# A float32 attention and GLU block on one core: the second token pair takes its 64 leftover rows into the seven products (49 matmuls a chunk for 50), and VectorE's sum of two partial results becomes an accumulation in PSUM

## The chip, the core and the metric

The kernel runs on one core of a Trainium2 chip. The engines of that core work side by side: TensorE (PE; its weight loads are listed apart as PEld) multiplies matrices and writes to PSUM, VectorE (DVE) and ScalarE (ACT) do elementwise work, GpSimd (POOL) does small tensor work and issues some of the transfers, and SyncE (SP) issues the other transfers. Each engine takes its instructions in a fixed order, which the builder of the program has laid down, and waits at an instruction until the semaphores that it needs are set. The metric is the device time of one execution in microseconds (us).

## What is computed

```python
x = A_x                                            # 1 x 2048 x 576, float32
h = x + A_ref(layernorm(x), wqkv, wo)              # 32 heads of 18, 8 keys at distance 2 behind each token
h2 = h + B_ref(layernorm(h), w_gate, w_up, w_down)

def B_ref(x, w_gate, w_up, w_down):                # 576 -> 4608 -> 576
    g = x @ w_gate
    u = x @ w_up
    return (sigmoid(g) * u) @ w_down
```

## The kernel before, in words

**Precision.** Every float32 operand of a large product is split into a high part that TensorE can take (`float32r`) and the low part that is left over: ScalarE copies the high part (L104), VectorE subtracts it from the source (L105). A product of two such operands takes three matmuls: high with high, low with high, high with low.

**Blocks and chunks.** The 2048 tokens are four blocks of 512. The 4608 hidden columns are 36 chunks of 128. The 576 input rows are four tiles of 128 and 64 rows over, the rest. For the rest the 64 rows stand twice in the 128 partitions, as high part and as low part, and two matmuls with the weights' high and low part cover it.

**Four stages of the second half.** The list `items` runs over 12 chunks of block 0 alone ("std"), 24 chunks of blocks 0 and 1 together (the first pair), 12 chunks of block 2 alone, and all 36 chunks of blocks 2 and 3 together (the last pair). In a pair, gate and up of two blocks are four outputs, and the function `pair` makes them by a scheme of seven products of half the inner length in place of eight: sums and differences of the operands are multiplied, and partial results are shared. The products are called by the names of their weights: b00, b10, t2, t3, t1, t4, b11. Each product is two tiles of 128 rows times three matmuls, 6 matmuls of 128 x 512 (`prod`, L747); the rests of the four outputs are added outside the scheme, by 4 x 2 matmuls (`rest`, L754). That makes 7 x 6 + 8 = 50 a chunk.

**Around the products.** The results stand in three PSUM tiles, b1, b2 and b3. ScalarE copies partial results out of them (L824, L834, L838), VectorE adds others to these copies (L829, L843, L848), ScalarE takes the sigmoid, and VectorE multiplies gate by up (L767; in the last pair L1187). In the last pair the down projection runs over two chunks at a time with seven products of its own (`down_seven`, L930: 14 steps of 6 matmuls of 128 x 288 for each half of the tokens in two chunks, results to the tile ev by ScalarE at L936, added to a buffer in HBM by transfers that GpSimd issues at L939). The other stages use `down_tile` (L868; PSUM tile dp), whose results ScalarE (L876) or VectorE (L878) take out.

**Preparing the operands.** The weights of the next chunk are prepared while this one runs (`weights`: four splits, and three subtractions at L727, L728, L730, from the tile wg that SyncE loads at L702). The operands of the last pair come from blocks 2 and 3, whose attention output is projected and normalised in the background of the third stage (`under_rest`, `proj_scr`, ending with ScalarE's writes to the tile ar at L978). From them `operands` makes the sums s1 to s4 (L281 to L287, and the rest's difference rd at L289) and splits seven operands, three of them with a rest (L108, L109).

**What sets the order.** The code is written as generators that are stepped between products (`between`, `bg_step`, `units`); priorities (HC above HI above none) and a list scheduler lay down each engine's order when the program is built. Buffers of a tile rotate: a new tile waits until the readers of the one that stood in its place are done.

## Time and profile before

| | |
|---|---|
| median of 3 runs | 1567.01 us (1566.04 to 1567.74) |
| profiled execution | 1568.13 us, of which 1566.4 us from the first to the last instruction |
| granted TensorE clock | 0.999 |
| PE busy / PEld busy | 1542.5 us / 1373.7 us |
| DVE busy / ACT busy / POOL busy | 1253.5 us / 874.0 us / 207.1 us |
| moved | 273.96 MB, 175 GB/s |

The span is a little shorter than the execution's time, since the time has the start and the end of the program in it as well. "Busy" is the union of an engine's instructions. Matmuls overlap in the records: one of 128 x 512 is listed with 391 ns, while the next one starts about 0.23 us after it. A line of groups gives the source line, engine, operation, output and inputs, shapes and count, then busy time and the mean of one instruction in ns, and behind the second bar the idle time of the engine just before them and what ended it.

### The profile page before, as it was taken

Reading aid. Unit: us, or ns where it says so; the run is one execution under the profiler, and the core shown is the slowest. Engines: PE = TensorE matmul, PEld = TensorE weight load, DVE = VectorE, ACT = ScalarE, POOL = GpSimd, SP = SyncE. Lnnn points to the kernel's source line nnn. Section 1 sums busy time; section 2 is a strip of 40 time slices with the busy share of each in tenths; the row PEclk is TensorE's granted clock in tenths of the full one; section 3 lists DMA queues with packets and bytes.
Section 4 is the critical chain, followed back from the end, with each engine's and each line's share of the span. In section 5 each row is a group of like instructions: output and inputs, shape, how many; then the busy total and the mean of one; then the engine's idle time right before and its main releaser. Section 6 shows DMA issues by size and latency. Waiting matters only on the chain.

```text
span 1566.4 us, 22385 instructions
## 1 busy us (share of the span) xinstructions
PE 1542.5 (98%) x8520; PEld 1373.7 (88%) x8520; DVE 1253.5 (80%) x1880; ACT 874.0 (56%) x1584; POOL 207.1 (13%) x252
## 2 busy tenths in 40 slices
PE   8999999999999999999999999999999999999998
PEld 7899888887888888888888888888888888888888
DVE  6998999969999999999526588866777776677754
ACT  6632245435656555666542355766677766677761
POOL 2300000011000110001101010112121121111212
PEclk9999999999999999999999999999999999999999
DMA  8646545266566776665683424898888889888984
GB/s 279 211 173 211 202 186 192 100 220 212 121 186 167 184 183 160 165 161 117 170 243 128 175 81 127 186 189 177 167 177 190 183 164 191 177 161 187 190 167 136
DMA packets 77148, 273.96 MB, mean 175 GB/s; under 512 B 8336, under 2 KB 14224, under 8 KB 76144
## 3 DMA queue, kind: packets, MB, share of 16 engines
q0 software_dynamic: 28192, 107.29, 37.4%
q1 hardware_dynamic: 41216, 145.11, 27.0%
q10 hardware_dynamic: 7632, 20.12, 3.4%
q8 instruction: 66, 1.08, 0.3%
q14 instruction: 42, 0.34, 0.1%
HBM read 143.98 MB, written 130.87 MB: 175 GB/s over the span
## 4 chain that ended last, share of the span: by engine, by line
PE 83%; DVE 8%; DMA 5%; ACT 1%; issue 1%; POOL 0%; ACTq 0%; SPq 0%; POOLq 0%; DVEq 0%
PE b L747 41%; PE dp L868 15%; PE dp L930 11%; PE b L754 8%; PE acc L157 4%; DMA wg<-in_wmlp_dram 2%; DVE pr L189 1%; DVE lg L193 1%; DVE pr L215 1%; PE b L157 1%; PE bgp L157 1%; DMA kw<-k 1%; DMA x<-tok 1%; DMA k<-ev 1%; DVE w L105 0%
## 5 line engine op out<-in xcount | busy, mean ns | idle before, releaser
L747 PE MATMUL b<-tl,w 128*128 128x512 f32 x1692 | 423.4, 392 | 1.6 <-ACT s L824 1.0
L747 PEld LDWEIGHTS b<-tl,w 128*128 128x128 f32 x1692 | 307.6, 188 | 59.7 <-ACT s L824 1.5
L747 PE MATMUL b<-th,w 128*128 128x512 f32 x1332 | 341.4, 391 | 0.4 <-DVE s L843 0.4
L747 PEld LDWEIGHTS b<-th,w 128*128 128x128 f32 x1332 | 246.0, 188 | 48.9 <-DVE s L843 0.8
L754 PE MATMUL b<-th,w 128*128 128x512 f32 x564 | 174.6, 390 | 0.0
L939 POOL DMA_DIRECT2D h<-ev x128 | 109.2, 853 | 455.9 <-ACT ev L936 451.0
L104 ACT ACTIVATE w<-wg 128x384 fp32r<-128x384 f32 (+1 forms) x186 | 111.0, 600 | 91.2 <-PE b L754 47.3
L157 PE MATMUL acc<-qw,th 128*128 128x432 f32 x512 | 154.3, 362 | 3.1 <-DVE th L109 2.3
L936 ACT ACTIVATE ev<-dp 128x576 f32<-128x576 f32 x224 | 139.0, 648 | 22.0 <-PE dp L930 22.0
L105 DVE TENSOR_TENSOR w<-wg,w 128x384 fp32r<-128x384 f32 (+1 forms) x186 | 120.9, 655 | 37.3 <-ACT w L104 37.1
L105 DVE TENSOR_TENSOR w<-tw,w 128x512 fp32r<-128x512 f32 x120 | 82.5, 688 | 79.6 <-ACT w L104 79.3
L754 PEld LDWEIGHTS b<-th,w 128*128 128x128 f32 x564 | 105.9, 188 | 22.5
L104 ACT ACTIVATE w<-tw 128x512 fp32r<-128x512 f32 x120 | 75.6, 630 | 83.4 <-PE b L747 82.3
L868 PE MATMUL dp<-d,h1h 128*128 128x288 f32 x640 | 118.8, 295 | 0.0
L868 PE MATMUL dp<-d,h0h 128*128 128x288 f32 x608 | 112.3, 295 | 0.0
L876 ACT ACTIVATE stage<-dp 128x576 f32<-128x576 f32 x104 | 66.9, 646 | 68.3 <-PE dp L868 68.1
L157 PEld LDWEIGHTS acc<-qw,th 128*128 128x128 f32 x512 | 96.7, 189 | 8.8 <-DVE th L109 3.4
L868 PEld LDWEIGHTS dp<-d,h1h 128*128 128x128 f32 x640 | 98.8, 189 | 3.0
L868 PEld LDWEIGHTS dp<-d,h0h 128*128 128x128 f32 x608 | 94.0, 189 | 3.5 <-DVE stage L878 0.3
L157 PE MATMUL acc<-qw,tl 128*128 128x432 f32 x256 | 92.8, 362 | 0.1
L189 DVE TENSOR_TENSOR pr<-kw,q 128x2304 f32<-128x2304 f32 x32 | 81.8, 2556 | 10.9 <-DMA kw<-k 10.7
L884 POOL DMA_DIRECT2D h<-stage x26 | 31.1, 1197 | 416.6 <-ACT stage L876 337.6
(323 smaller groups left out, 2971.6 us busy)
## 6 DMA issues: line engine op xcount, KB each, us to landing
h<-ev POOLq DMA_DIRECT2D x96, 576.0 KB, 7.1
wg<-in_wmlp_dram SPq DMA_DIRECT2D x47, 928.0 KB, 5.2
h<-stage POOLq DMA_DIRECT2D x26, 1152.0 KB, 11.7
wg<-in_wmlp_dram SPq DMA_DIRECT2D x36, 640.0 KB, 5.3
kw<-k SPq DMA_DIRECT2D x16, 792.0 KB, 5.1
vw<-v SPq DMA_DIRECT2D x16, 792.0 KB, 5.1
wd<-in_wmlp_dram SPq DMA_DIRECT2D x18, 576.0 KB, 8.1
h<-ev POOLq DMA_DIRECT2D x32, 288.0 KB, 5.1
```

What stands on the lines that cost most here:

```text
L104: act.activation(hi, src, AF.Copy)
L105: splits.append(dve.tensor_tensor(lo, src, f32(hi), ALU.subtract))
L157: pe.matmul(ps[:, :n], a[:, c, js], m[:, c], start=k == 0, stop=False)
L189: dve.tensor_tensor(pr, both(kw, u), q[:, us].unsqueeze(2).broadcast_to([P, 2, W, CG]), ALU.mult)
L747: pe.matmul(ps, wt[:, a, k0 + c], xx[:, m + c], start=first and k == 0, stop=k == 5, skip_group_check=True)
L754: pe.matmul(ps, wt[:, a, k0], xx[:, 4], start=False, stop=a == 1, skip_group_check=True)
L868: pe.matmul(ps[:, i, :DH2], a[:, js], d[:, m, i * DH2:(i + 1) * DH2], start=k == 0, stop=k == n)
L876: act.activation(hv, ps, AF.Copy)
L884: pool.dma_start(hacc[b], hs, accum_op=ALU.add, max_dma_last_dim=8 * D)
L930: pe.matmul(ps[:, i, :DH2], a[x][:, js], m[y], start=k in (0, 1, 3) and q == 0, stop=q == 2, skip_group_check=True)
L936: act.activation(hs[:, k % 2], ps[:, :, :DH2], AF.Copy)
L939: pool.dma_start(hsev[:, u, k0:k + 1], hs[:, :k + 1 - k0], accum_op=ALU.add, max_dma_last_dim=8 * D)
```

## The change

- Only the last pair is given new weights and operands. The 64 rows of the rest are cut into two halves of 32 rows, one for each half of the inner length, and so take part in the scheme of seven products. In the 128 partitions the token operand of a rest holds its 32 rows as high, low, high, high; the weight operand holds high, high, low, low, of which the last is zero, so that one matmul gives the three terms. Each product is 6 + 1 matmuls: 7 x 7 = 49 a chunk (`product`, `full_weights`).
- A second packing of the weights, `wfull`, is an input of its own, with 12 x 128 columns a chunk in place of 10 x 128. The preparation of a chunk's weights works in place in the loaded tile, with six copies on ScalarE and twelve operations on VectorE for four and seven.
- The seven operands of the last pair each have a rest. The rest rows of blocks 2 and 3 are written to HBM (`rscr`, GpSimd's queue, 2 transfers of 128 KB) and read back into four tiles rr00 to rr11, the 32 rows four times over (16 transfers of 64 KB on the same queue). `x_full` and `split_quads` split each rest with one copy on ScalarE and one subtraction on VectorE of 32 partitions.
- In both pairs the products stand in another order: b00, t3, t2, b10, t1, t4, b11. From the second chunk of each pair on, ScalarE copies b00's result from one PSUM tile into the other (the new L895), the matmuls of b10 (eight in the first pair, seven in the last) accumulate on top of it, and the sigmoid reads PSUM; VectorE's addition L829 is gone there. The first chunk of each pair keeps the addition (the new L910).
- Buffers: s has 3 for 4, ev has 3 for 4, d3 has 1 for 2. The rests of the token operands have a pool of their own. A chunk's first copy of weights waits for the last sigmoid of the chunk before it.

The diff, cut to its core:

```diff
+    rscr = [dr.tile([DR, TB], F32, name=f"r{b}") for b in (2, 3)]
...
+    def split_quads(t, src):
+        act.activation(t, src, AF.Copy)
+        dve.tensor_tensor(t[32:64], src[32:64], f32(t[32:64]), ALU.subtract)
...
+    def full_weights(ws):
+        r = ws[:, :GF].rearrange("p (b c n) -> p b c n", b=4, c=3)
+
+        def quads(t, src):
+            act.activation(t, src, AF.Copy)
+            dve.tensor_tensor(t[64:128], src[64:128], f32(t[64:128]), ALU.subtract)
+
+        def sum_pair(name, q, bs):
+            t = gw.tile([P, 2, 4, P], F32R, name=name)
+            split(t[:, :, 0:2], t[:, :, 2:4], r[:, bs, 1:3])
+            quads(tr[:, q:q + 2], r[:, bs, 0])
+            return t
+
+        with tc.high_priority(HI):
+            w1 = gw.tile([P, 2, 5, P], F32R, bufs=2, name="w1")
+            with ExitStack() as way:
+                if c >= NF + NSTD:
+                    way.enter_context(tc.issue_after(added[1]))
+                act.activation(w1[:, :, 0:3], r[:, 2:4], AF.Copy)
+            dve.tensor_tensor(w1[:, :, 3:5], r[:, 2:4, 1:3], f32(w1[:, :, 1:3]), ALU.subtract)
+            dve.tensor_tensor(w1[64:128, :, 0], r[64:128, 2:4, 0], f32(w1[64:128, :, 0]),
+                              ALU.subtract)
+            dve.tensor_tensor(r[:, 1], r[:, 0], r[:, 1], ALU.subtract)
+            dve.tensor_tensor(r[:, 2], r[:, 1], r[:, 2], ALU.add)
+            dve.tensor_tensor(r[:, 3], r[:, 3], r[:, 2], ALU.subtract)
+            tr = gw.tile([P, 8, P], F32R, tag="tw", name="tr")
+            w2 = sum_pair("w2", 0, slice(1, 3))
+            w4 = gw.tile([P, 6, P], F32R, name="w4")
+            act.activation(w4[:, 0:3], r[:, 0], AF.Copy)
+            dve.tensor_tensor(w4[:, 3:5], r[:, 0, 1:3], f32(w4[:, 1:3]), ALU.subtract)
+            dve.tensor_tensor(w4[64:128, 0], r[64:128, 0, 0], f32(w4[64:128, 0]), ALU.subtract)
+            dve.tensor_tensor(r[:, 0], r[:, 0], r[:, 2], ALU.subtract)
+            w3 = sum_pair("w3", 2, slice(0, 4, 3))
...
+    def product(ps, n, xn, w, first, rests):
+        prod(ps, X[xn], w, n, first)
+        if isinstance(w[n][1], int):
+            for m, wn in rests:
+                rest(ps, X[m], w, wn)
+        else:
+            pe.matmul(ps, w[n][1], XR[xn], start=False, stop=True, skip_group_check=True)
...
-        prod(b1, X["a00"], w, "b00", True)
+        product(b1, "b00", "a00", w, True, ())
         with tc.high_priority(HC):
-            act.activation(s1, b1, AF.Copy)
+            act.activation(b2 if clean else s1, b1, AF.Copy)
         between(0)
-        prod(b2, X["a01"], w, "b10", True)
-        rest(b2, X["a01"], w, "g4")
+        product(b3, "t3", "s3", w, True, ())
...
+        product(b2, "b10", "a01", w, not clean, (("a01", "g4"),))
         with tc.high_priority(HC):
-            act.activation(s3, b3, AF.Copy)
+            if clean:
+                act.activation(s1, b2, AF.Sigmoid)
+            else:
+                dve.tensor_tensor(s1, s1, b2, ALU.add)
+                act.activation(s1, s1, AF.Sigmoid)
...
+        elif b > 1:
+            pool.dma_start(rscr[b - 2], raw[0:DR, 4])
...
+            rr = [[pp.tile([P, TB], F32, name=f"rr{i}{h}") for h in range(2)] for i in range(2)]
+            for i in range(2):
+                for h in range(2):
+                    a = rscr[i][32 * h:32 * h + 32, :]
+                    for q in range(4):
+                        pool.dma_start(rr[i][h][32 * q:32 * q + 32], a)
+                    yield
...
-                    hs = st.tile([P, 2, 2, DH2], F32, bufs=4, name="ev")
+                    hs = st.tile([P, 2, 2, DH2], F32, bufs=3, name="ev")
```

Three places show what the change does to the order of an engine's instructions. (In these lists w1 to w4 are the split weights of a chunk, tr their rests for t1 to t4, th and tl operands with and without a rest, xa00 and xs1 to xs3 the new rests of the token operands; the number behind a name tells one tile from the next of the same name.)

**TensorE in a chunk of the last pair.** Before, the second chunk, whole: b00 in the bank b2_9212, b10 in b3_9213, and so on, with four rests of two matmuls.

```order
L747 MATMUL b2_9212<-tl_8832,w1_9031 128x512 x6
L747 MATMUL b3_9213<-th_8835,w1_9031 128x512 x6
L754 MATMUL b3_9213<-th_8835,w1_9031 128x512 x2
L747 MATMUL b2_9212<-tl_8892,w2_9035 128x512 x6
L747 MATMUL b1_9214<-tl_8895,w2_9035 128x512 x6
L747 MATMUL b2_9212<-tl_9019,w3_9036 128x512 x6
L754 MATMUL b2_9212<-th_9022,w4_9034 128x512 x2
L747 MATMUL b1_9214<-th_9022,w3_9036 128x512 x6
L754 MATMUL b1_9214<-th_9022,w1_9031 128x512 x2
L747 MATMUL b2_9212<-th_8904,w4_9034 128x512 x6
L754 MATMUL b2_9212<-th_8904,w4_9034 128x512 x2
```

Now, the end of the second chunk (t2, b10, t1, t4, b11) and the first product of the third:

```order
L808 MATMUL b1_9251<-tl_8901,w2_9065 128x512 x6
L818 MATMUL b1_9251<-xs2_8902,tr_9064 128x512
L808 MATMUL b2_9253<-th_8913,w1_9057 128x512 x6
L818 MATMUL b2_9253<-th_8913,w1_9057 128x512
L808 MATMUL b1_9251<-tl_9042,w3_9075 128x512 x6
L818 MATMUL b1_9251<-xs1_9043,tr_9064 128x512
L808 MATMUL b3_9252<-th_9048,w3_9075 128x512 x6
L818 MATMUL b3_9252<-th_9048,tr_9064 128x512
L808 MATMUL b1_9251<-th_8933,w4_9070 128x512 x6
L818 MATMUL b1_9251<-th_8933,w4_9070 128x512
L808 MATMUL b2_9389<-tl_8859,w1_9226 128x512 x6
L818 MATMUL b2_9389<-xa00_8860,w1_9226 128x512
```

The pairs of rest matmuls have become one matmul behind each product.

**TensorE at the join of the third stage and the last pair.** Before, from t1 of the first chunk (bank b1_9049) to t2 of the second, where each bank is finished before the next chunk begins:

```order
L747 MATMUL b1_9049<-tl_9019,w3_8941 128x512 x6
L754 MATMUL b1_9049<-th_9022,w4_8939 128x512 x2
L747 MATMUL b3_9051<-th_9022,w3_8941 128x512 x6
L754 MATMUL b3_9051<-th_9022,w1_8936 128x512 x2
L747 MATMUL b1_9049<-th_8904,w4_8939 128x512 x6
L754 MATMUL b1_9049<-th_8904,w4_8939 128x512 x2
L747 MATMUL b2_9212<-tl_8832,w1_9031 128x512 x6
```

Now, the same place: the first chunk has the banks b1_9084, b2_9082, b3_9083, the second b1_9251 and b3_9252.

```order
L808 MATMUL b1_9251<-tl_8859,w1_9057 128x512 x6
L818 MATMUL b1_9251<-xa00_8860,w1_9057 128x512
L818 MATMUL b3_9083<-xs3_8880,tr_8959 128x512
L808 MATMUL b3_9083<-th_9048,w3_8970 128x512 x6
L818 MATMUL b3_9083<-th_9048,tr_8959 128x512
L818 MATMUL b2_9082<-xs2_8902,tr_8959 128x512
L808 MATMUL b2_9082<-tl_9042,w3_8970 128x512 x6
L818 MATMUL b2_9082<-xs1_9043,tr_8959 128x512
L808 MATMUL b3_9252<-tl_8879,w2_9065 128x512 x4
L808 MATMUL b2_9082<-th_8933,w4_8965 128x512 x6
L818 MATMUL b2_9082<-th_8933,w4_8965 128x512
L808 MATMUL b3_9252<-tl_8879,w2_9065 128x512 x2
```

The rests of t3 and t2 of the first chunk now stand behind b00 of the second chunk, each right ahead of the next product into the same bank. Behind the last row come one matmul more of the second chunk's t3 (its rest) and the first matmul of the down projection (`dp` from h0h), which needs the first chunk's gate times up.

**VectorE at the same place.** Before, from the last operand (a11, the tile th_9022) to the addition behind b10 and on:

```order
L105 TENSOR_TENSOR th_9022<-ar3_8328,th_9022 128x1024
L878 TENSOR_TENSOR stage_7678<-stage_7678,dp_9062 128x576
L105 TENSOR_TENSOR w1_9031<-wg_8952,w1_9031 128x640
L727 TENSOR_TENSOR tw_9037<-wg_8952 128x512
L829 TENSOR_TENSOR s_9052<-s_9052,b2_9050 128x512
L109 TENSOR_TENSOR th_9022<-ar3_8328,th_9022 64x512
L878 TENSOR_TENSOR stage_7678<-stage_7678,dp_9088 128x576
```

Now, from a11's rest on:

```order
L115 TENSOR_TENSOR th_9048<-rr11_8819,th_9048 32x512
L758 TENSOR_TENSOR wg_8975<-wg_8975 128x384
L107 TENSOR_TENSOR w2_9065<-wg_8975,w2_9065 128x2x256
L951 TENSOR_TENSOR stage_7657<-stage_7657,dp_9142 128x576
L756 TENSOR_TENSOR wg_9080<-wg_9080 128x384
L1108 TENSOR_TENSOR rd_8815<-rr10_8818,rr11_8819 128x512
L910 TENSOR_TENSOR s_9085<-s_9085,b1_9084 128x512
L1108 TENSOR_TENSOR rr10_8818<-rr00_8816,rr10_8818 128x512
L951 TENSOR_TENSOR stage_7657<-stage_7657,dp_9165 128x576
L115 TENSOR_TENSOR xs3_8880<-rr10_8818,xs3_8880 32x512
L115 TENSOR_TENSOR xs1_9043<-rd_8815,xs1_9043 32x512
```

The work on the rests stands behind the last operand's main part, among the sums of the down results (L878, now L951) and the weights of the second and third chunk. From the sum s1 (before L281, now rs0) up to the row of xs3 there are 52 instructions now: 9 of 1024 columns, 8 of 576, 18 of 512, 10 of 384, 6 of 256 and 1 of 128.

More of the change, by code (lines that the diff above doesn't have):

```diff
@@ L60, with kernel @@
 @with_exitstack
-def kernel(ctx, tc, x, wqkv, wo, wmlp, out):
+def kernel(ctx, tc, x, wqkv, wo, wmlp, wfull, out):
     nc = tc.nc
@@ L298, in tl_tile, with x_full @@
         return xt.tile([P, 4, TB], F32R, tag="tl", bufs=4, name="tl")
+    def x_full(n, raw, rest):
+        if n in ("a01", "a11", "s4"):
+            t = th_tile()
+            r = t[:, 4]
+        else:
+            t = tl_tile()
+            r = xr.tile([P, TB], F32R, name="x" + n)
+        split(t[:, 0:2], t[:, 2:4], raw)
+        split_quads(r, rest)
+        XR[n] = r
+        return t
+    XR = {}
+    xr = None
     def x_half(raw, rest):
@@ L698, with load_gu @@
         gw.tile([P, n, P], F32 if name == "tw" else F32R, name=name)
[L700 removed]
+    def load_gu(f, full):
         ws = gw.tile([P, WC], F32, bufs=2, name="wg")
[L702 removed]
+        n, src = (GF, wfull) if full else (WC, wmlp)
+        behind[0] = sp.dma_start(ws[:, :n], src[f][:, :n])
         return ws
@@ L746, in prod @@
             for a, m in ((0, 0), (0, 2), (1, 0)):
-                pe.matmul(ps, wt[:, a, k0 + c], xx[:, m + c], start=first and k == 0,
+                lhs = wt[:, a, k0 + c] if isinstance(k0, int) else wt[:, 2 * a + c]
+                pe.matmul(ps, lhs, xx[:, m + c], start=first and k == 0,
                           stop=k == 5, skip_group_check=True)
                 k += 1
+    def product(ps, n, xn, w, first, rests):
[5 more added lines that the diff above has]
+            pe.matmul(ps, w[n][1], XR[xn], start=False, stop=True, skip_group_check=True)
     def rest(ps, xx, w, n):
@@ L849, in pair @@
             gated[0] = act.activation(s2, s2, AF.Sigmoid)
+            added[1] = getattr(gated[0], "ins", gated[0])
         between(5)
-        prod(b1, X["s4"], w, "b11", False)
-        rest(b1, X["s4"], w, "u4")
         with tc.high_priority(HC):
-            last((s1, b1), (s2, s3))
+            last(1, s2, s3)
+        product(b1, "b11", "s4", w, False, (("s4", "u4"),))
+        with tc.high_priority(HC):
+            last(0, s1, b1)
         between(6)
@@ L1292, in between @@
                 side(i)
-            pair(X, w, between, last)
+            pair(w, between, last)
         else:
@@ L1309, in between @@
                 down_side(f, i)
-            pair(X, w, between, last if f >= NF - NPL else last_sums(f))
+            pair(w, between, last if f >= NF - NPL else last_sums(f))
             if f < NF - NPL:
```

123 lines of the change are left out of this document (79 added, 44 removed).

## The prediction

> **What bounds the kernel now.** I read the page first, then the groups and the stretches of the last pair, then its chain, then the join ahead of it.
>
> ```profile
> span 1566.4 us, 22385 instructions
> PE 1542.5 (98%) x8520; PEld 1373.7 (88%) x8520; DVE 1253.5 (80%) x1880; ACT 874.0 (56%) x1584; POOL 207.1 (13%) x252
> ```
>
> TensorE is busy for 98% of the span. Whether that is a bound must be seen in the stage that the change touches most. Of 1077 to 1281 us, twelve chunks of the last pair, the groups of TensorE say:
>
> ```profile
> L747 PE MATMUL b<-tl,w 128*128 128x512 f32 x288 | 71.8, 391 | 0.0
> L747 PE MATMUL b<-th,w 128*128 128x512 f32 x216 | 55.1, 390 | 0.0
> L754 PE MATMUL b<-th,w 128*128 128x512 f32 x96 | 29.7, 390 | 0.0
> ```
>
> 288 + 216 + 96 = 600 matmuls in 12 chunks, the 50 a chunk of the scheme, and no idle time ahead of any. Their 390 ns overlap; what one costs is read from the chain of waits, where there is nothing but matmuls in this stretch:
>
> ```profile
> 1183.80 1.60 PE dp L930 x12
> 1188.04 2.75 PE b L747 x12
> 1192.83 2.73 PE b L747 x12
> 1205.03 2.75 PE b L747 x12
> ```
>
> 2.73 / 12 = 0.2275 us for one of 128x512, 1.60 / 12 = 0.133 us for one of the down projection. 50 x 0.2275 + 42 x 0.133 = 16.97 us, and from the second row to the last, one chunk, it is 16.99 us. So a chunk of the last pair is the sum of its matmuls, with nothing else in it. The stretches (in the order PE, PEld, DVE, ACT, POOL busy, clock, DMA share, GB/s) show where that holds and where not:
>
> ```profile
> 340.00:420.00 80.00, 76.84 (x412) 65.07 (x412) 73.19 (x111) 42.97 (x73) 11.34 (x16) 1.00 0.56 172
> 920.00:940.00 20.00, 20.00 (x108) 17.51 (x108) 19.54 (x28) 11.78 (x19) 0.00 (x0) 1.00 0.21 67
> 940.00:958.00 18.00, 18.00 (x102) 15.97 (x101) 13.05 (x21) 6.54 (x12) 1.23 (x1) 1.00 0.42 120
> 958.00:990.00 32.00, 32.00 (x157) 27.23 (x157) 31.59 (x58) 22.17 (x41) 1.76 (x2) 1.00 0.56 134
> 1077.00:1281.00 204.00, 204.00 (x1107) 179.45 (x1106) 148.44 (x259) 143.14 (x259) 40.93 (x48) 1.00 0.88 178
> ```
>
> In the steady last pair (last row) TensorE is full, VectorE has 12.37 us of work in a chunk, ScalarE 11.93. At the join (rows two to four) TensorE is full too, but VectorE has only 70 - 64.2 = 5.8 us to spare from 920 to 990 us. At the head of the first pair (first row) TensorE loses 3.2 us.
>
> **Matmuls removed.** One in each of 36 chunks of the last pair: 36 x 0.2275 = 8.2 us, all on the path. The first pair keeps its 50, so its chunks cannot become shorter where TensorE is full.
>
> **Weights of a chunk in the last pair.** The prices by form, VectorE first, then ScalarE; the last ScalarE rows are from 920 to 950 us:
>
> ```profile
> L105 DVE TENSOR_TENSOR w<-tw,w 128x512 fp32r<-128x512 f32 x24 | 16.5, 689 | 28.3 <-ACT w L104 28.3
> L105 DVE TENSOR_TENSOR w<-wg,w 128x640 fp32r<-128x640 f32 x12 | 9.8, 819 | 0.0
> L829 DVE TENSOR_TENSOR s<-s,b 128x512 f32<-128x512 f32 x12 | 8.3, 688 | 10.2 <-PE b L754 9.8
> L727 DVE TENSOR_TENSOR tw<-wg 128x512 f32<-128x512 f32 x12 | 8.2, 687 | 0.0
> L105 DVE TENSOR_TENSOR w<-wg,w 128x384 fp32r<-128x384 f32 x12 | 6.6, 553 | 0.0
> L730 DVE TENSOR_TENSOR tw<-wg,tw 128x256 f32<-128x256 f32 x12 | 5.0, 419 | 0.0
> L104 ACT ACTIVATE w<-tw 128x512 fp32r<-128x512 f32 x24 | 15.2, 634 | 24.3 <-PE b L747 24.3
> L104 ACT ACTIVATE w<-wg 128x640 fp32r<-128x640 f32 x12 | 8.7, 722 | 0.0
> L824 ACT ACTIVATE s<-b 128x512 f32<-128x512 f32 x12 | 7.1, 594 | 1.7 <-PE b L747 1.7
> L104 ACT ACTIVATE w<-wg 128x384 fp32r<-128x384 f32 x12 | 6.3, 525 | 5.6 <-PE b L754 5.6
> L104 ACT ACTIVATE tl<-rs 128x1024 fp32r<-128x1024 f32 x2 | 2.1, 1054 | 1.0 <-DVE rs L283 1.0
> L104 ACT ACTIVATE w<-wg 128x256 fp32r<-128x256 f32 x1 | 0.4, 418 | 0.3 <-PE b L747 0.3
> ```
>
> VectorE loses 0.82 + 0.55 + 2 x 0.69 + 0.69 + 2 x 0.42 and the addition L829, 0.69: 4.97 us. It gains three operations of 512 columns, four of 384, and five of 256 or fewer: 3 x 0.69 + 4 x 0.55 + 5 x 0.42 = 6.37. Net +1.4, so 13.8 us in a chunk of 16.77. ScalarE loses 0.72 + 0.53 + 2 x 0.63 = 2.5 and gains 768 columns (between 0.72 and 1.05, by columns 0.83), 0.53, 2 x 0.63 and 2 x 0.42 = 3.46: 12.9 of 16.77. Both stay at about 80% and under TensorE: no cost. Their cover is the slack of a chunk; the tightest edge is tr, one buffer for four rests, free after t4 and needed by the next chunk's t3, two products and a down step later, 2 x 1.6 + 0.8 = 4.0 us, against a copy and a subtraction of 0.42 each. If that cover went, each us would cost 36 us.
>
> **Accumulation in PSUM.** The trace has no copy of ScalarE from PSUM to PSUM; nearest is L824, PSUM to SBUF, 0.59 us. Its bounds are 0.42 and 1.05 us, the ends of the ScalarE rows above. t2 waits for it behind six or more matmuls of t3, 1.37 us, so only the upper end leaves too little for the two handovers; L834 before had the same cover (t2, then t3, then t1) and made no idle time in the steady part. I take 0. VectorE's 23 additions less in the first pair, 16 us, lie beside a full TensorE and bring nothing there; only the 3.2 us lost at 340 to 420 us could shrink. Gain 3.2 at most, loss about 1.5 (half of it again, since the new order falls differently among the long attention operations); I take 0.
>
> **The join.** The last operand data is written here, and the rests then leave by GpSimd's queue:
>
> ```profile
> 919.83 0.26 ACT L978 ACTIVATE ar<-bgp 128x128 f32<-128x128 f32 x1
> 896.49 0.74 POOL L976 DMA_DIRECT2D h<-hj  x1 [35.96 <-DVE hj L262]
> h<-hj POOLq DMA_DIRECT2D x8, 288.0 KB, 2.6
> 920.02 0.42 DVE L105 TENSOR_TENSOR w<-wg,w 128x256 fp32r<-128x256 f32 x1
> 920.35 1.22 DVE L281 TENSOR_TENSOR rs<-ar 128x1024 f32<-128x1024 f32 x1
> 921.49 0.69 DVE L767 TENSOR_TENSOR s<-s,b 128x512 f32<-128x512 f32 x1
> 922.08 0.56 DVE L105 TENSOR_TENSOR w<-wg,w 128x384 fp32r<-128x384 f32 x1
> 922.55 1.22 DVE L283 TENSOR_TENSOR rs<-rs,ar 128x1024 f32<-128x1024 f32 x1
> 940.28 1.54 PE L747 MATMUL b<-tl,w 128*128 128x512 f32 x6
> ```
>
> One write and 16 reads (the first read stands ahead of the write) at 0.74 us of issue each are 17 x 0.74 = 12.6 us, and the last lands 2.6 us later: 920.1 + 12.6 + 2.6 = 935.3 us. GpSimd has nothing else to do there (0.00 in the second stretch). VectorE is the later one. From start to start an operation of 1024 columns takes 1.14 us, of 512 0.59, of 384 0.47, of 256 0.33; between them one of 576 is 0.67 and one of 128 about 0.2. The 52 instructions from the sum s1 to the rest of s3 are 9 x 1.14 + 8 x 0.67 + 18 x 0.6 + 10 x 0.47 + 6 x 0.33 + 0.2 = 33.3 us, from 920.35 to 953.7. TensorE starts the last pair at 940.28 (last row) and has in front of t3's rest three products of seven, two of six and four groups of down matmuls: 21 x 0.2275 + 12 x 0.2275 + 4 x 1.60 = 13.9 us, to 954.2. So this rest is just in time. Behind it three waits are new, because no down work is left to fill them. t4 goes into the bank of t3's rest and needs ScalarE's copy in between, 0.6 us and 0.2 for the handovers. t1 behind t2's rest, the same: 0.8. The first down matmul needs VectorE's product and ScalarE's copy behind b11, 0.69 + 0.63 + 0.25, and has three matmuls of t3 to cover it, 0.7: 0.9. Together 2.5 us. Below: nothing is to be gained, since TensorE has no idle time there before; the low end is 0. Above: VectorE has five rest splits and three sums more, 8 x 0.6 = 4.8 us, and the weights of three chunks, 3 x 1.4 and the L829 that the first chunk keeps, 4.9. That is 9.7 against 5.8 to spare, and 3.9 may come on top: 6.4 us. I take 2.5, by the three waits.
>
> **Buffers.** ev with 3 for 4: in the last pair a transfer of ev and the third tile after it stand like this, the second row being two copies of which the second opens that tile at 1197.2:
>
> ```profile
> 1189.47 0.85 POOL L939 DMA_DIRECT2D h<-ev  x1 [3.04 <-ACT ev L936]
> 1196.62 1.21 ACT L936 ACTIVATE ev<-dp 128x576 f32<-128x576 f32 x2
> h<-ev POOLq DMA_DIRECT2D x96, 576.0 KB, 7.1
> DMA to landing us min/median/max: 4.6/6.3/9.4
> q1 hardware_dynamic: 8979, 29.45, 16.4%
> ```
>
> The room is 7.7 us, the landing 7.1 in the middle and 9.4 at most, so ScalarE will sometimes wait, up to 1.7 us. TensorE needs that bank only two products and a step later, 4.0 us: no cost. The loads grow by 0.131 MB a chunk; in 1009 to 1519 us 29.45 MB took 16.4% of 510 us (last row: packets, MB, share), 2.8 us a MB: +0.37 us to 0.88 x 17.0 = 15.0 us of transfer in a chunk of 16.77, 91%.
>
> **Sum.** -8.2 + 2.5 = -5.7 us: against the profiled execution 1568.13 - 5.7 = 1562.4. The median of the runs before, 1567.01, is 1.1 us lower than that execution, so 1561.3. About 0.2%, 3.1 us, is what a measurement can tell from no change.
>
> **A rule weighed.** TensorE's weight loads are busy for 179.45 of 204 us, 88%, with no idle time before any matmul. The Trainium skill, Perfetto Trace Analysis, section Identifying the Most-Contended Engine, says that busy matmuls are a bad measure of how near TensorE is to its limit, and that the busy share of weight loads is a better one. By it 12% would be free, something else would be the bound, and a matmul less would bring nothing: 1567 in place of 1561. The chain, 16.99 us for 16.97 of matmuls, decides against it here; what is left of it is a rival.
>
> **Rivals.**
> - The join costs nothing (VectorE's rests come earlier, or the new waits overlap): 1567.0 - 8.2 = 1558.8, and with the head of the first pair repaired 1555.6. For it: the margin at 954 us is within the error of my count. Against: each new wait is in TensorE's own order.
> - The join costs its upper end, VectorE being late with all that it has over: 1567.0 - 8.2 + 6.4 = 1565.2, no change. For it: 31.59 of 32 us busy at 958 to 990.
> - The removed matmuls were not the bound, and each chunk stays at 17.0 us: 1567.0 + 2.5 = 1569.5 at most, no change. Against it: the chain.
> - Slower, by ev: if a landing goes beyond 7.7 + 4.0 - 0.65 = 11 us, TensorE waits for the bank, once in two chunks, 17 times; beyond 11.5 us, 0.52 us each time, that is 8.8 us and outweighs the 5.7 by 3.1: from there slower, at 12 us 1578. For it: a queue at 91%. Against it: 9.4 is the longest now.
> - Slower, by the rests: were each transfer to wait until the one ahead has landed, 17 x 2.6 = 44 us would put the last at 964, ten behind the need: 1571. Against it: ev's transfers are issued every 4.2 us and land after 7.1, so they overlap. The Trainium skill, DMA: Bandwidth & Descriptors, section Anatomy of one DMA, gives a fixed 2.0 us and bytes / 436e3 for one such transfer; one behind the other these would make an estimated 37 us, to 957.
>
> **Chances.** My forecast (join 1 to 4 us) 0.50; free join 0.22; dear join 0.13; not the bound 0.04; ev 0.07; rests 0.04. Faster takes the first two, 0.72; the next two are the same, 0.17; slower 0.11. The range from 1557.0 to 1566.5 holds the forecast, most of the free join and the dear join, and leaves out the two slower cases, the fourth and the gain at the first pair's head. The forecast's own range is 1559.5 to 1563.5.
>
> **What would show it.** Chunks of the last pair 16.75 us apart in the chain; 588 matmuls in twelve of them, with idle 0.0; VectorE near 13.8 and ScalarE near 12.9 us a chunk; TensorE idle for 1 to 4 us between 940 and 975, behind ACT copies of b and ahead of the first dp; the rests' reads landed by 936. ScalarE waiting on ev's transfers for some tenths of a us a chunk, and TensorE not. It is wrong if TensorE shows idle time in each chunk, or if the lost time at the join, or at the head of the first pair, is over 6 us.

## The result, and the profile after

The changed kernel is 1.3% slower: 1586.69 us median of 6 runs (1579.91 to 1592.66) against 1566.01 us, ratio 1.0133, 95% interval 1.0104 to 1.0161. The prediction was 1561.3 us. The runs spread over 13 us, those of the kernel before over 4. The profiled execution took 1592.66 us, the slowest of the six, so the stalls below are at their larger end.

The head of the page of the kernel after, and the shares of its engines in the chain of work that ended last:

```profile
span 1590.9 us, 22470 instructions
PE 1551.7 (98%) x8484; PEld 1373.8 (86%) x8484; DVE 1297.4 (82%) x2009; ACT 906.7 (57%) x1660; POOL 218.3 (14%) x270
PE 58%; DVE 24%; DMA 12%; ACT 3%; issue 2%; POOL 0%; SPq 0%; ACTq 0%; DVEq 0%; POOLq 0%
```

TensorE has 36 matmuls less (8484 for 8520) and yet 9 us more of busy time. Before the change, DMA had 5% of the chain; now it has 12%. Where that happens is seen in the stretches (PE, PEld, DVE, ACT, POOL busy, clock, DMA share, GB/s). First the kernel before: the head of the first pair, the join, the even part of the last pair. Then the same of the kernel after:

```profile
340.00:422.00 82.00, 78.84 (x424) 66.93 (x424) 75.19 (x114) 44.97 (x76) 11.34 (x16) 1.00 0.54 168
940.00:985.00 45.00, 45.00 (x231) 38.80 (x230) 39.71 (x68) 26.13 (x48) 2.14 (x2) 1.00 0.45 116
985.00:1526.00 541.00, 541.00 (x2923) 475.27 (x2922) 388.99 (x676) 376.95 (x679) 108.27 (x127) 1.00 0.89 181
```

```profile
340.00:422.00 82.00, 78.66 (x425) 66.73 (x424) 75.64 (x113) 46.00 (x78) 11.32 (x16) 1.00 0.57 177
942.00:997.00 55.00, 49.89 (x229) 40.46 (x228) 47.94 (x85) 30.03 (x56) 2.27 (x3) 0.94 0.40 106
997.00:1551.00 554.00, 543.73 (x2888) 471.64 (x2887) 437.04 (x806) 403.42 (x744) 109.06 (x127) 0.99 0.89 184
```

The first pair is as it was. The join takes 55 us for 45, with TensorE idle for 5.1 us and a clock of 0.94. The even part of the last pair takes 554 us for 541; TensorE was full there and is now idle for 10.3 us, spread over it, and runs at half its clock for 6.8 us of it.

**The even part.** Of 1009 to 1519 us, the waits of the kernel after (us in total, times, longest), and the group of L756, the first subtraction in the newly loaded weights:

```profile
DVE wg L756 <- DMA wg<-in_wfull_dram: 79.1, 25, 7.7
PEld b L808 <- DVE s L915: 6.9, 6, 2.3
PEld dp L1003 <- DVE d L107: 6.0, 7, 1.3
L756 DVE TENSOR_TENSOR wg<-wg 128x384 f32<-128x384 f32 x29 | 16.2, 558 | 79.3 <-DMA wg<-in_wfull_dram 79.1
```

VectorE stands still for 79 us at one instruction. In the kernel before no instruction of VectorE or ScalarE waited for a load of weights in this stretch. The chain at one such place, and TensorE's row there:

```profile
1137.47 9.52 DMA wg<-in_wfull_dram
1147.08 0.10 DVE wg L756
1147.56 0.69 DVE s L915
1148.29 2.05 PE b L808 x6
1148.29 2.05 PE L808 MATMUL b<-th,w 128*128 128x512 f32 x6 [2.02 <-DVE s L915]
```

The load of the weights, wg, is issued at 1137.47 us and lands 9.52 us later. L756 stands in VectorE's fixed order ahead of L915, the addition that reads the bank b1; b11 goes into that bank next, so TensorE waits 2.02 us. The transfers themselves are hardly different: from issue to landing 4.3, 5.3 and 8.7 us (least, median, most) in the kernel before, 4.1, 5.3 and 9.5 after. What changed is the time between the issue and the first reader. Before, the first reader of the load issued at 1103.86 us was a copy of ScalarE at 1115.95 us, 12.1 us later:

```profile
1103.86 0.33 SPq L702 DMA_DIRECT2D wg<-in_wmlp_dram  x1
1115.95 0.72 ACT L104 ACTIVATE w<-wg 128x640 fp32r<-128x640 f32 x1
1109.69 0.56 DVE L756 TENSOR_TENSOR wg<-wg 128x384 f32<-128x384 f32 x1 [3.98 <-DMA wg<-in_wfull_dram]
```

The third row is the kernel after: its load left at 1103.89 us, and L756 had been waiting for 3.98 us when it could start, 5.8 us behind the issue.

**The join.** The chain there, the last pieces ahead of the first down matmul of the last pair, and above it, as the first row, the first two loads of the down weights in the kernel before:

```profile
940.40 0.90 SPq L1145 DMA_DIRECT2D wd<-in_wmlp_dram  x2
957.68 1.56 PE b L808 x6
959.24 7.51 DMA wd<-in_wmlp_dram
966.84 1.02 ACT d L106 x2
...
968.75 0.53 ACT h0h L106
969.32 0.61 PE dp L1003
```

The first load of the last pair's down weights, wd, left at 940.40 us before the change and leaves at 959.24 now. SyncE waits 11.2 us at it, by the trace for VectorE's L115, which splits a rest. The pool `dw`, from which wd comes, is opened over the memory of the operands' pool, and the new tiles of the rests (rr, rd), which lie at that pool's end, are read until about 959 us. ScalarE's copies of wd stand ahead of its copy h0h, which the first down matmul needs.

### The profile page after: what moved, and what is told of

It is laid out like the page before. It is cut to its first block, busy times and chain, and to the rows that moved or that the text cites. A ratio compares the mean times of both kernels' runs of the same rounds, so it can differ in the third digit from the quotient of the medians.

```text
span 1590.9 us, 22470 instructions
## 1 busy us (share of the span) xinstructions
PE 1551.7 (98%) x8484; PEld 1373.8 (86%) x8484; DVE 1297.4 (82%) x2009; ACT 906.7 (57%) x1660; POOL 218.3 (14%) x270
## 4 chain that ended last, share of the span: by engine, by line
PE 58%; DVE 24%; DMA 12%; ACT 3%; issue 2%; POOL 0%; SPq 0%; ACTq 0%; DVEq 0%; POOLq 0%
PE b L808 27%; PE dp L941 13%; DMA wg<-in_wfull_dram 7%; PE dp L1003 5%; PE acc L163 4%; PE b L823 3%; DMA wg<-in_wmlp_dram 2%; DVE d L107 2%; PE b L818 2%; DVE w L107 2%; DVE pr L195 2%; DVE lg L199 1%; DVE r L1296 1%; DVE pr L221 1%; PE b L163 1%
## 5 line engine op out<-in xcount | busy, mean ns | idle before, releaser
L808 PE MATMUL b<-tl,w 128*128 128x512 f32 x1692 | 431.4, 394 | 2.6 <-DVE tl L107 1.2
L808 PE MATMUL b<-th,w 128*128 128x512 f32 x1332 | 346.3, 395 | 6.5 <-DVE s L915 5.8
L808 PEld LDWEIGHTS b<-th,w 128*128 128x128 f32 x1332 | 247.5, 189 | 58.8 <-DVE s L915 7.4
L106 ACT ACTIVATE w<-wg 128x384 fp32r<-128x384 f32 (+2 forms) x186 | 111.9, 604 | 119.1 <-PE b L823 34.0
L107 DVE TENSOR_TENSOR w<-wg,w 128x384 fp32r<-128x384 f32 (+2 forms) x186 | 121.2, 655 | 47.5 <-ACT w L106 47.1
L756 DVE TENSOR_TENSOR wg<-wg 128x384 f32<-128x384 f32 x36 | 20.1, 558 | 85.8 <-DMA wg<-in_wfull_dram 85.6
L823 PE MATMUL b<-th,w 128*128 128x512 f32 x276 | 85.7, 390 | 0.0
L221 DVE TENSOR_TENSOR pr<-vw,lg 128x2304 f32<-128x2304 f32 x32 | 81.8, 2556 | 0.8
L199 DVE TENSOR_REDUCE lg<-pr 128x128 f32<-128x2304 f32 x32 | 81.5, 2548 | 0.3
```

Source lines behind the costliest of these rows:

```text
L106: act.activation(hi, src, AF.Copy)
L107: splits.append(dve.tensor_tensor(lo, src, f32(hi), ALU.subtract))
L199: dve.tensor_reduce(lg[:, us].rearrange("p j w h -> p (j w h)"), pr.rearrange("p j w (h d) -> p (j w h) d", d=DH), AX.X, ALU.add)
L221: dve.tensor_tensor(pr.rearrange("p j w (h d) -> p j w h d", d=DH), both(vw, u).rearrange("p j w (h d) -> p j w h d", d=DH), lg[:, us].uns ...
L808: pe.matmul(ps, lhs, xx[:, m + c], start=first and k == 0, stop=k == 5, skip_group_check=True)
L823: pe.matmul(ps, wt[:, a, k0], xx[:, 4], start=False, stop=a == 1, skip_group_check=True)
```

## The experiments

All ratios are to the kernel before the change, run on the same chip; 0.001 is 1.6 us. "Kernel 4" is the kernel of experiment 4; in the forecasts the kernel of the three edits is kernel 4, that of the four edits kernel 6.

**1. The first reader held back.** VectorE's L756 stands behind w1's rest instead of ahead of it:

```diff
-            dve.tensor_tensor(w1[:, :, 3:5], r[:, 2:4, 1:3], f32(w1[:, :, 1:3]), ALU.subtract)
+            up = dve.tensor_tensor(w1[:, :, 3:5], r[:, 2:4, 1:3], f32(w1[:, :, 1:3]), ALU.subtract)
...
-            dve.tensor_tensor(r[:, 1], r[:, 0], r[:, 1], ALU.subtract)
+            with tc.issue_after(getattr(up, "ins", up)): dve.tensor_tensor(r[:, 1], r[:, 0], r[:, 1], ALU.subtract)
```

> The changed kernel with one edit: VectorE's first reader of a new weight load (L756, the difference of two columns) is held behind the rest of w1 (L753), some 5 us later in VectorE's order; the same work otherwise. Theory A (in the last pair the load is issued when the tile before it has been read out, lands 5 to 9.5 us later, and L756 stands in VectorE's order 5.8 us behind the issue and ahead of the additions that TensorE waits for): VectorE's wait for the load, 79 us in 1009 to 1519 us, falls below 10 us, TensorE's lost time in the last pair's even part, about 20 us, falls below 4, and the time falls from 1587 by 13 to 20 us, to 1567 to 1574. Theory B (VectorE and ScalarE have too much work in a chunk, or the transfers of ev with three buffers hold ScalarE): the wait moves to another instruction and the time stays within 4 us of 1587.

1573.66 us median of 10 runs, ratio 1.0039 (1.0024 to 1.0054): 0.0094 or 15 us less than the changed kernel, with about 5 us either way. The group of L756 in 1009 to 1519 us, and the stretch of the even part:

```profile
L756 DVE TENSOR_TENSOR wg<-wg 128x384 f32<-128x384 f32 x30 | 16.7, 558 | 0.4
985.00:1526.00 541.00, 541.00 (x2920) 473.47 (x2919) 447.51 (x822) 413.36 (x757) 109.21 (x127) 1.00 0.91 188
```

The wait is gone and TensorE is full again. The first reader of a load is now a copy of ScalarE (L752), at 1112.31 us for a load issued at 1101.67, 10.6 us behind it. VectorE does the same work as before the edit: 419 us for 30 chunks' L756 from 1009 to 1519 us, where it was 406 us for 29. So it was the place of one instruction in an engine's order, not too much work: theory A.

**2. The hidden sums moved away from the stage tile.** In the changed kernel the first product of the join, L1296, waits 2.10 us for the landing of the old stage tile, over which its output lies:

```diff
-                    for n in ("s4h", "s4l", "s1h"):
+                    for n in ("s4h", "s4l", "s1h", "s1l", "s3l"):
```

> The changed kernel with one edit: two more names are reserved at the start of the pool of the last pair's hidden sums, so that the first products r10 and r00 lie outside the old stage tile, whose accumulating transfer is still under way at the join. Theory A (the 8 KB of the new rests push that pool down onto the stage tile; the first product waits 2.1 us for the landing at 965.7, and with it tr, h0h and TensorE, whose clock then halves for 5 us): VectorE's wait at 963.7 to 965.7 goes, TensorE's idle time at 965 to 970 us falls from 4.3 to below 2, the slow matmuls behind it go, and the time falls by 4 to 7 us, to 1580 to 1583. Theory B (VectorE's work at the join alone makes TensorE late): the wait goes, the idle time stays, and the time falls by less than 2 us.

1588.9 us, ratio 1.0146 (1.0117 to 1.0176): nothing gained. The wait for the stage tile is gone, but the first down matmul still waits, now in one piece (the waits of 935 to 1000 us):

```profile
PEld dp L1003 <- ACT h0h L106: 4.0, 1, 4.0
ACT d L106 <- DMA wd<-in_wmlp_dram: 3.9, 1, 3.9
```

My first reading of the join was wrong: two landings end within 1.1 us of each other (965.7 the stage, 966.8 wd), and taking away the earlier one changes nothing.

**3. Edits 1 and 2 together.**

> The changed kernel with both edits, the first reader of a load held back and the two names reserved. Theory A: what they bring adds up, 17 to 26 us, to 1561 to 1570: about the time before. What is left against the 8.2 us of the removed matmuls is then the lateness of the operands' rests at 953 to 960 us, 3 to 4 us, and the third stage's 1.5: 1562 to 1564 is the likeliest. Theory B: above 1580.

1572.87 us, ratio 1.0041 (1.0025 to 1.0057), the same as edit 1 alone: the two do not add up as theory A had it.

**4. The rests' tiles first in their pool**, on top of 3, so that wd lies over the sums and not over the rests:

```diff
-        s = [pp.tile([P, 2, TB], F32, name=f"rs{i}") for i in range(3)]
+        rr = [[pp.tile([P, TB], F32, name=f"rr{i}{h}") for h in range(2)] for i in range(2 * p)]
         rd = pp.tile([P, TB], F32, name="rd")
+        s = [pp.tile([P, 2, TB], F32, name=f"rs{i}") for i in range(3)]
         if p == 1:
-            rr = [[pp.tile([P, TB], F32, name=f"rr{i}{h}") for h in range(2)] for i in range(2)]
```

> The kernel with both edits (first reader of a load held back, two names reserved) and a third: in the operands' pool of the last pair the tiles of the rests (rr and rd) are allocated ahead of the sums rs, so that the pool of the down weights, opened behind it, lies over the sums alone and no longer over the rests. Theory A' (at the join two transfers hold the first down matmul, and the later one decides: the first load of the down weights waits 11 us on SP's queue for the last reader of a rest's buffer, is issued at 957 to 959 us in place of 940, lands 7.7 us later, and ScalarE's copy of it stands ahead of h0h, which the first down matmul needs; the landing of the stage tile is the other, 1 us earlier): with both gone the load is issued by 945, TensorE's idle time ahead of the first down matmul falls from 3.8 to about 1 us, the half-speed stretch behind it, 1.5 us, goes, and the time falls by 4 to 6 us from 1573 to 1567 to 1569. Theory B (VectorE's work at the join is the limit): less than 2 us.

1570.8 us median of 12, ratio 1.0015 (1.0003 to 1.0027), 0.0026 or 4.1 us less than 3, with about 3 us either way. The load leaves at 952.71 us for 956.99, not by 945 as I had expected (it is now behind the load of a chunk's weights on SyncE's queue), and that is enough. First the row of kernel 3, then of this one:

```profile
967.24 0.40 PE L1003 MATMUL dp<-d,h0h 128*128 128x288 f32 x1 [3.68 <-ACT h0h L106]
971.66 0.40 PE L1003 MATMUL dp<-d,h0h 128*128 128x288 f32 x1 [1.20 <-ACT h0h L106]
```

**5. Edits 1 and 4 without 2.**

> The first reader held back and the rests' tiles ahead of the sums, but without the two reserved names: the load of the down weights is early, the wait for the stage tile's landing (965.7 us) is there. Theory A': the later of two landings decides, so one alone brings less than 1.5 us: 1571 to 1574. If the load of the down weights was the only thing that mattered: 1567 to 1569.

1572.4 us, ratio 1.0028 (1.0018 to 1.0039): 1.7 us less than 1 and 2 us more than 4, by the intervals told apart from neither. The trace puts it between the two: VectorE waits 1.4 us for the stage tile again, and from the first matmul of the last pair to the first of its sixth chunk it takes 85.6 us, where kernel 1 takes 86.9 and kernel 4 takes 83.0. That fits two landings of which the later one decides; one trace of each kernel is behind it.

**6. The sums of the rests early**, on top of 4:

```diff
-                dve.tensor_tensor(qo, qx, qy, op)
+                with tc.high_priority(HC): dve.tensor_tensor(qo, qx, qy, op)
```

> The kernel of the three edits and a fourth: the sums of the rests (the second instruction of each sum of operands) get the highest priority on VectorE. Theory A' and the new waits (t4 behind the copy of t3's rest, t1 behind that of t2's, 0.96 and 0.62 us in the run before, and 1.1 us where the sigmoid's addition stands behind other work of VectorE): rests come up to 4 us earlier, the two waits go or fall to half, and the time falls by 1 to 2 us more, to 1565 to 1568. Theory B, that VectorE is full there, makes it no better: what comes earlier pushes other work back, 0 to 2 us worse.

1567.33 us median of 12, ratio 0.9998 (0.9985 to 1.0011): 2.7 us less than 4 by the ratios (3.3 with about 2 either way by the mean of the 12 runs of each, taken on one chip), and as fast as the kernel before the change. What TensorE still waits for at the join:

```profile
940.02 1.66 PE L808 MATMUL b<-tl,w 128*128 128x512 f32 x6 [0.68 <-DVE s L836]
945.87 1.20 PE L808 MATMUL b<-tl,w 128*128 128x512 f32 x4 [0.60 <-DVE w L107]
957.37 1.65 PE L808 MATMUL b<-th,w 128*128 128x512 f32 x6 [0.17 <-DVE s L915]
963.42 0.40 PE L1003 MATMUL dp<-d,h0h 128*128 128x288 f32 x1 [0.96 <-ACT h0h L106]
```

**7. The same one priority lower** (HI for HC).

> The kernel of the four edits with the sums of the rests one step lower in VectorE's order, level with the splits of the operands and below the additions of the pair. In the kernel of the four edits TensorE is idle at the join for 0.84, 0.76, 0.33 and 1.48 us; the first two stand behind weights' rests (w2, L758) and the addition of b10 that the sums of the rests have pushed back. Theory (VectorE is full from 920 to 960 us, and its order there only shares out the lateness): the first two shrink, the third grows, together within 1 us: 1566 to 1569, no difference that can be measured. Rival (order alone is at fault): both go, 1565 to 1566, faster than before the change by 0.1%.

1568.17 us, ratio 1.001 (1.0000 to 1.0020): not told apart from 6. That fits the theory that the order of VectorE's work there only shares out the lateness, but it was shared out otherwise than forecast: the first of the four waits above is 0.75 us in this trace, the second 0.42, the third is gone and the last is 0.91, 2.1 us together for 2.4. (The forecast's figures are larger, since they count from start to start and not from the listed end of a matmul.)

**8. A fiftieth matmul again**, on top of 4: t3's rest twice.

```diff
-            pe.matmul(ps, w[n][1], XR[xn], start=False, stop=True, skip_group_check=True)
+            for _ in range(2 if n == "t3" else 1):
+                pe.matmul(ps, w[n][1], XR[xn], start=False, stop=True, skip_group_check=True)
```

> The kernel of the three edits with one matmul more in each chunk of the last pair: t3's rest is multiplied twice (its value is then wrong; nothing else changes), 50 matmuls a chunk as before the change. Price of a matmul on the path: 36 x 0.2275 = 8.2 us more than the kernel of the three edits if TensorE is again the bound of the last pair; 0 to 3 us if something else is (VectorE, ScalarE or the transfers).

1579.39 us, ratio 1.0071 (1.0056 to 1.0085): 0.0056 or 8.8 us more than 4, with about 3 us either way. One matmul a chunk is on the path and costs its full time, 8.8 / 36 = 0.24 us.

**9. Without PSUM seeding**, first in the changed kernel, then in kernel 6:

```diff
-        clean = order[3:]
+        clean = []
```

> The changed kernel without PSUM seeding: every chunk of the pairs copies b00's product to s1 and VectorE adds b10's, as before the change; matmuls, weights and rests as in the changed kernel. Theory A (seeding costs nothing; its copy of 0.58 to 0.60 us is the price that was taken): VectorE gets 58 additions of 0.69 us back; in the first pair, full TensorE, nothing moves (within 2 us), in the last pair one more instruction stands behind the late load, so 1585 to 1595. Theory C (the copy from PSUM to PSUM makes TensorE wait, or the banks that it takes do): faster than 1582.

1592.12 us, ratio 1.0156 (1.0140 to 1.0173), against 1.0133 (1.0104 to 1.0161) of the changed kernel: not told apart by the intervals.

> The kernel of the four edits (1567.3 us) without PSUM seeding: VectorE does the addition of b00 and b10 in every chunk of the pairs. Without seeding the changed kernel was 5 us slower, with the late loads still in it. Theory A (there the additions cost only because they stood behind a late load): 0 to 2 us more now, 1567 to 1569. Theory C' (seeding is worth those 5 us by itself, VectorE having no room for the additions in the last pair): 1571 to 1574, with TensorE idle in the even part.

1582.15 us, ratio 1.0089 (1.0073 to 1.0104), 14 us more than kernel 6. Both theories missed the size. With the loads in time, seeding is worth more than the removed matmuls bring. VectorE's row in the even part of the two kernels, first without seeding, then with:

```profile
985.00:1526.00 541.00, 537.68 (x2864) 463.88 (x2864) 454.88 (x838) 398.30 (x741) 108.31 (x126) 1.00 0.90 185
985.00:1526.00 541.00, 541.00 (x2912) 473.12 (x2911) 444.77 (x816) 410.72 (x752) 109.76 (x128) 1.00 0.92 190
PEld dp L1003 <- DVE d L107: 6.8, 14, 0.5
PEld dp L1003 <- ACT d L106: 5.4, 14, 0.7
```

VectorE is busy for only 84% without seeding, and yet TensorE waits once in two chunks (the last two rows, of 1009 to 1519 us), behind the split of the down weights d. The addition L910 stands on the chain of work that ended last, ahead of that split, at 1188.50 and again at 1222.94 us, two chunks later. So a chunk takes 17.22 us where it takes 16.86 in kernel 6 (experiment 10), and 36 x 0.36 = 13 us are nearly all of the 14. Why the same edit cost nothing that could be told in the kernel with late loads was not shown; VectorE waited there for 79 us anyhow, which may have taken the additions in (without seeding that wait is 57.5 us).

**10. What makes the matmuls wider.** A chunk of kernel 6 takes 16.86 us, not the 16.75 of the sum. In two kernels on top of 6 the rest matmul reads other data of the same size: the first tile of the operand's main part for the rest's columns, then the first tile of the product's main weights for the rest's weights.

> The kernel of the four edits; the rest matmul of every product reads the first tile of the operand's main part in place of the stacked rest (its value is wrong; as many matmuls of the same size). For the width of a matmul: the mean start-to-start of one of 512 columns in the even part is 228.7 ns before the change and 230.6 after it, and the 7th matmul of a product takes 226 where it reads the operand's own tile and 231 to 234 where it reads a tile of its own, with an uneven row behind it (226, 236, 228, 233, 231). If reading another tile for the rest's columns does that: a mean of 228.5 to 229.2, and 3 us less. If not: 230.4 to 230.8.

> The same question for the weights: the rest matmul of every product loads the first tile of that product's main weights in place of the rest's (value wrong, as many matmuls). If another tile for the rest's weights makes the row uneven: a mean of 228.5 to 229.2 ns, and 3 us less. If not: 230.4 to 230.8.

The mean start-to-start of a matmul of 512 columns from 1000 to 1500 us (some 1450 of them; holes, where it is over 300 ns, left out) is 228.7 ns before the change, 230.6 in kernel 6, 228.7 with the operand's own tile, 230.4 with the product's own weights. The times, 1569.41 and 1573.17 us, are single runs and decide nothing. The chunks do; down steps one chunk apart in the chains of kernel 6, of kernel 8 and of the one with the operand's own tile:

```profile
1180.33 1.57 PE dp L1003 x12
1197.19 1.57 PE dp L1003 x12
```

```profile
1180.37 1.59 PE dp L1004 x12
1197.46 1.59 PE dp L1004 x12
```

```profile
1188.94 1.60 PE dp L1003 x12
1205.71 1.60 PE dp L1003 x12
```

16.86 us, 17.09 with the fiftieth matmul (kernel 8 is built on kernel 4, whose chunk takes 16.86 as well), and 16.77 where the rest's columns come from the tile that the product reads anyway.

## Why the prediction was wrong, step by step

- **Weights of a chunk, "no cost": this step failed.** Its sums were right. The even part of kernel 6:

```profile
989.00:1525.00 536.00, 536.00 (x2888) 468.93 (x2887) 439.85 (x808) 406.74 (x745) 108.39 (x126) 1.00 0.92 190
```

Over 536 / 16.86 = 31.8 chunks that is 13.8 us of VectorE and 12.8 of ScalarE a chunk, for 13.8 and 12.9 forecast. But a sum says only that there is room. I looked at the edges on TensorE's side (tr) and not at the one towards the load: what reads a load first, how long behind its issue, and what stands behind that reader in its engine's order. The trace of before had both numbers, 12.1 us from the issue to the first reader and up to 8.7 to the landing; the new order of VectorE shows L756 ahead of L915. It cost 15 us (experiment 1, about 5 either way).
- **The join, 2.5 us with ends 0 and 6.4: mis-sized, and outside its ends.** It cost 10 us. The rests landed earlier than forecast, by 932.4 us and not 935.3 (an issue took 0.50 us, not 0.74). The two waits of t4 and t1, forecast at 0.8 each, were there at 0.69 each (first two rows below). The third, the first down matmul, was forecast at 0.9; in the kernel after it is 1.51 + 1.81 us, since two transfers that the sum did not contain end there. Experiment 4 gives 4.1 us for them and the slow clock behind them, experiment 6 another 2.7 for VectorE's lateness, and some 3 us are left. The traces agree: from the first matmul of the last pair to the first of its sixth chunk they show 77.6 us before the change, 86.9 after it, 87.1 in kernel 3, 83.0 in kernel 4 and 80.4 in kernel 6. That what is left comes near my 2.5 is partly luck. In kernel 4 the three waits of the sum are there, 0.69, 0.46 and 1.20 us, with 0.56 and 0.95 us behind VectorE's additions beside them; in kernel 6 only the first down matmul's, 0.96, is one of the three.

```profile
957.68 1.66 PE L808 MATMUL b<-th,w 128*128 128x512 f32 x6 [0.69 <-ACT s L899]
960.49 1.65 PE L808 MATMUL b<-tl,w 128*128 128x512 f32 x6 [0.69 <-ACT s L903]
967.00 0.51 PE L818 MATMUL b<-xs,tr 128*128 128x512 f32 x1 [1.51 <-DVE tr L739]
969.32 0.61 PE L1003 MATMUL dp<-d,h0h 128*128 128x288 f32 x1 [1.81 <-ACT h0h L106]
```

- **Matmuls removed, -8.2 us: right in kind, mis-sized.** The fiftieth matmul costs 8.8 (about 3 either way). But the 49 that stay are wider, 230.6 ns for 228.7: 16.99 - 16.86 = 0.13 us a chunk in place of 0.23, 4.7 us in place of 8.2. The Trainium skill, Perfetto Trace Analysis, section Identifying the Most-Contended Engine, takes the busy share of weight loads as a better measure of TensorE's limit; that share is 473.12 of 541 us, 87%, in kernel 6, and a matmul more costs its full time all the same, so the rival drawn from it does not hold here.
- **Accumulation in PSUM, 0:** right for what the step covered, the copy's own price (0.59 us in the group of the new L895) and the first pair (78.66 us busy for 78.84 at its head). Not said was what the cover is worth: without seeding kernel 6 loses 14 us (about 3 either way), 13 of them in the last pair by its chunks.
- **Buffers of ev, 0:** right. ScalarE waited on ev's transfers 1.2 us in 510 in the kernel after, 4.2 in kernel 6, and TensorE not for them.
- **The rivals:** neither slower case was the one that came, which had been in none of my sums. Both asked whether a transfer comes late, not whether a reader had moved towards the transfer.

Together, from 1.0133: 15 us of late first readers, 4 of the late landings at the join, 2.7 of VectorE's order there. With them gone the change is worth nothing that can be measured (0.9998): its 8.2 us are spent on wider matmuls, 36 x (16.86 - 16.77) = 3.2 us, on what is left at the join, some 3 us, and the rest is within the interval of 2 us.

## What to carry to other kernels

Where a change reorders the preparation of loaded data, measure the lead of each load, from issue to first reader, against the longest landing in the trace, and then read what stands behind that reader on its engine: an engine busy for 80% still holds the next one up if its head waits. Where a change adds tiles, see which pool is opened later over their memory and which transfer that holds back; of two waits that end together, taking away the earlier one shows nothing. An addition that VectorE need not make can be worth time though VectorE is busy for only 84%: here 0.36 us a chunk for an addition of 0.69, because work that TensorE needs stood behind it.

## What the hardware showed

**Half speed behind short holes.** After TensorE's idle time at the join its clock fell to one half. The stretches of 5 us in the kernel after:

```profile
965.00:970.00 5.00, 1.67 (x6) 0.73 (x5) 3.80 (x8) 2.92 (x6) 0.00 (x0) 0.85 0.46 180
970.00:975.00 5.00, 5.00 (x12) 3.98 (x13) 4.17 (x9) 2.06 (x4) 0.00 (x0) 0.50 0.34 109
```

12 matmuls in 5 us, one every 0.427 us for 0.227: 2.4 us lost on top of the wait. The granted clock in the trace is one half from 968.49 to 975.32 us. The same followed the hole of 2.02 us that ended at 1148.29 us, shown above, from 1149.40 to 1152.81. At about 825 us, where the third stage has a hole in every run, the idle time was 1.82 us before the change and the matmuls behind it went at full speed; it was 1.96 us after it, and they were slow from 828.55 to 831.96 us. The first row is before, the second after, each followed by four down matmuls (0.69 and 1.16 us):

```profile
827.11 0.66 PE L146 MATMUL b<-ident,oj 128*128 128x128 f32 x4 [1.82 <-DVE tl L105]
829.73 0.69 PE L868 MATMUL dp<-d,h1h 128*128 128x288 f32 x4
827.09 0.66 PE L152 MATMUL b<-ident,oj 128*128 128x128 f32 x4 [1.96 <-DVE tl L107]
830.62 1.16 PE L941 MATMUL dp<-d,h1h 128*128 128x288 f32 x4
```

Length alone does not decide. In the fourteen traces, from 800 to 1555 us and leaving out the join, no hole of 1.72 to 1.83 us was followed by half speed (9 holes), and of those of 1.85 to 2.12 us 9 of 13 were, each for 3.41 us; behind the longest of them, 2.12 us at 830 us in the kernel with the operand's own tile, the clock stayed whole. So a wait of 2 us on TensorE can cost 3.7, and that may be why the runs of the changed kernel spread more; this is not shown. Part of the spread has nothing to do with the change: in five of the fourteen traces TensorE also ran at half speed for 6.83 us between 182 and 193 us, and the first matmul of `prod` came 222.4 to 225.6 us into the span, for 218.8 to 221.6 in the others. The Trainium skill, TensorE: Matmul & The Clock Gate, section Part 1: The HAM clock gate, tells of such a halving after an idle window of about 3.4 us that runs freely, and of as long a time at half speed. The trace agrees on the half and, with 3.41 us, on the length; the holes that were enough here, some 2 us, are shorter than that window, and why is open.

**Wider matmuls.** Matmuls whose columns come from another tile than those ahead of them in the product take 231 to 234 ns for 226, and the row behind is uneven (226, 236, 228, 233, 231 ns) where it was level; behind down matmuls it was as uneven before the change (237, 233, 232, 231). Experiment 10, with one trace of each kernel, shows that the tile of the columns does it and that of the weights does not; whether it is the address or the change of tile wasn't tried.
